# One in-place ring instead of two, and a TensorE loop with register addresses

## The chip, the cores and the metric

The kernel runs on one core of a Trainium2 chip. The core has five engines with instruction streams of their own, which meet only through semaphores: TensorE (PE) multiplies matrices, VectorE (DVE) and ScalarE (ACT) copy and compute, GpSimd (POOL) and SyncE (SP) here mostly issue transfers. Transfers between the chip's main memory and the on-chip memory run on 16 DMA engines that all queues share. The metric is the time of one execution on the device in microseconds, the median of several runs; lower is better.

## The reference

With the kernel size k = 1, the grouped convolution is a small matrix product for every pixel:

```python
H = W = 512; G = 4; Cg = 48; C = 192
x: (1, 512, 512, 192) bfloat16      w: (1, 1, 4, 48, 48) bfloat16
out[b, h, w, g, d] = sum over c of x[b, h, w, g, c] * w[0, 0, g, c, d]
```

That is 262,144 pixels of 192 channels in four groups of 48. Input and output have 100.7 MB each.

## The kernel before, in words

**Layout.** Pixels are laid out on the 128 partitions of the on-chip memory. A *column* is one pixel per partition, 384 bytes in each, so the input is about 2,056 columns. Four columns are a *group* g, two groups a *pair*. Nearly all columns lie in fields of 128 rows, where every partition reads one long run of main memory (`FULL`). Two narrow fields (`PARTIAL`, `UNEVEN` in `FRONT`) have only 120 rows, moved in several blocks of 16, 44, 12 and 32 rows, some issued by SyncE or ScalarE (the queue called "sync") and some by GpSimd. [...] Tiny transfers (`filler`, lines 282 to 287) stand between GpSimd's blocks[...].

**Two rings.** `ring` holds 240 columns of input in three slots of 80 (`BIG`, `SLOTS`), `oring` 280 columns of output. `plan_pieces` cuts the input into loads of 80 columns (8, 24 and 48 at the start), `plan_stores` the output into stores of about 70 (smaller at the end: 28, 24, 20, 16, 8).

**TensorE** (lines 322 to 397). For each pair, `transposes(pair)` turns two groups around, 12 transposes of 128x128 into `xT_ps`, each a weight load from `ring` and a matmul with the identity. `matmuls(pair)` multiplies the turned data by the weights, 12 matmuls into `o_ps`. `step(pair)` does the transposes of the next pair, then the matmuls of this one. Nine pairs are written out, then a hardware loop (line 392) turns 8 times over 30 pairs, which is one whole turn of the ring, so that every address in its body is a constant; the rest is written out again. Before the first group of a slot PE waits for the load's semaphore (line 344) and takes its 16 off again with a later transpose (line 353).

**VectorE** copies each turned pair from `xT_ps` to `xT_sb` (line 409). **ScalarE** copies each group's result from `o_ps` to `oring` (line 446), issues the stores (line 427) one group late, and waits, before it writes over a place in `oring`, until the store that read it has landed (lines 416 to 420 and 444).

**SyncE** (lines 311 to 320) issues the loads in order; before each it waits for the transposes that free its slot (`freed`, line 264). **GpSimd** (lines 268 to 309), after making constants, does the blocks of the two narrow fields: it waits for the transposes, issues the loads, waits until all of them have landed, tells PE by one increment of the slot's semaphore (line 300), and later issues the stores of the field.

Of the kernel before, what the change touches and what calls it, by code (L numbers as in the profile page):

```python
# [24 lines left out]
BIG = 80  # L25
SLOTS = 3
RCOLS = SLOTS * BIG
OGRID = (72, 140, 212, 280)
OCOLS = OGRID[-1]
HEAD = (8, 24, 48)  # L30
LATE_COLS = 240
LATE_PART = 40
LAST_PARTS = (24, 20, 16, 8)
NXP = 4
NXS = 3
NOB = 4
NTOK = 6

FULL = (("sync", 0, 128, 128, 0),)

# [4 lines left out]
UNEVEN = (("sync", 0, 16, 4, 16), *PARTIAL[1:])  # L45
FRONT = ((6, ((48, PARTIAL), (32, FULL))), (11, ((48, UNEVEN), (32, FULL))))

# [4 lines left out]
class Field:  # L52


    def __init__(self, cols, blocks, g0, pix):
        self.cols, self.g0, self.g1 = cols, g0, g0 + cols // 4
        self.full = blocks is FULL
        self.blocks = []
        for (queue, r0, rows, outer, less) in blocks:
            self.blocks.append((queue, r0, rows, outer, pix, cols - less))  # L60
            pix += rows * (cols - less)
        self.pix_end = pix
        assert cols % 4 == 0


class Piece:

    def __init__(self, i, field, c0, size):
        self.i, self.field = i, field
        self.c0, self.c1, self.size = c0, c0 + size, size  # L70
        self.g0, self.g1 = field.g0 + self.c0 // 4, field.g0 + self.c1 // 4
        self.at = 4 * self.g0 % RCOLS
        self.full, self.blocks = field.full, field.blocks
        assert size % 4 == 0 and self.at + size <= RCOLS


class Store:

    def __init__(self, field, c0, c1, at):
        self.field, self.c0, self.c1, self.at = field, c0, c1, at  # L80
        self.g0, self.g1 = field.g0 + c0 // 4, field.g0 + c1 // 4


def plan_fields(npix):

    parts, head = [], sum(HEAD)
    for slots, special in FRONT:
        parts += [(head + BIG * slots, FULL), *special]
        head = 0
    cols = npix - sum((n - b[4]) * b[2] for n, blocks in parts for b in blocks)  # L90
    if cols < 128 * BIG:
        parts, cols = [], npix
    assert cols % 512 == 0
    fields, g, pix = [], 0, 0
    for n, blocks in [*parts, (cols // 128, FULL)]:
        fields.append(Field(n, blocks, g, pix))
        g, pix = fields[-1].g1, fields[-1].pix_end
    assert pix == npix
    return fields


def plan_pieces(fields):
    pieces = []
    for f in fields:
        first = [f.cols]
        if f.full:
            first = list(HEAD) if not f.g0 and sum(HEAD) <= f.cols else []
        c = 0
        while c < f.cols:
            n = first.pop(0) if first else min(BIG, f.cols - c)  # L110
            pieces.append(Piece(len(pieces), f, c, n))
            c += n
    return pieces


def plan_stores(fields):
    total = 4 * fields[-1].g1
    stores, at = [], 0
    for f in fields:
        c = 0  # L120
        if not f.full and at + f.cols > OCOLS:
            at = 0
        ends = []
        if f is fields[-1] and f.cols > LATE_COLS:
            ends = [f.cols - sum(LAST_PARTS[i:]) for i in range(len(LAST_PARTS))]
        while c < f.cols:
            if f.full:
                end = min([g for g in OGRID if g > at + 24] or [OCOLS]) - at + c
                if f.cols < BIG:
                    end = min(OCOLS - at + c, f.cols)  # L130
                if ends and c >= f.cols - LATE_COLS:
                    end = min(OCOLS - at, LATE_PART) + c
                end = min([end, f.cols] + [e for e in ends if e > c])
            else:
                end = f.cols
            stores.append(Store(f, c, end, at))
            c, at = end, (at + end - c) % OCOLS
    return stores


class Unit:


    def __init__(self, pieces):
        self.pieces, self.g0, self.g1 = pieces, pieces[0].g0, pieces[-1].g1
        self.slot = pieces[0].at // BIG
        self.regular = pieces[0].at % BIG == 0 and 4 * (self.g1 - self.g0) == BIG


def plan_units(pieces):  # L150
    units, rest = [], list(pieces)
    while rest:
        n = 1
        if rest[0].g0 and rest[0].at % BIG == 0:
            while n < len(rest) and rest[n].at % BIG:
                n += 1
        units.append(Unit(rest[:n]))
        rest = rest[n:]
    return units


def loop_spans(units):

    body, out, run = RCOLS // 4, [], []
    for u in units + [None]:
        if u and u.regular:
            run.append(u)
            continue
        if run:

            first = max((run[0].g0 - 1) // 2, 1)
            rounds = (run[-1].g1 - 2 * first - 2) // body
            if rounds > 1:
                out.append((first, body // 2, rounds))
        run = []
    return out


def bass_standalone__grouped__vision_kernel(nc, x, w, out):
# [3 lines left out]
    assert npix % 512 == 0, "the pixel count must be a multiple of 512"  # L183

    fields = plan_fields(npix)
    pieces = plan_pieces(fields)
    stores = plan_stores(fields)
    units = plan_units(pieces)
    unit_of = {g: u for u in units for g in range(u.g0, u.g1)}
    store_of = {g: s for s in stores for g in range(s.g0, s.g1)}  # L190
    NG = pieces[-1].g1
    NP = (NG + 1) // 2
    LOOPS = loop_spans(units)
    assert all(RCOLS // 4 % n == 0 for n in (2 * NXS, 2 * NTOK, NXP))

# [4 lines left out]
    def groups(pair):  # L200
        return range(2 * pair, min(2 * pair + 2, NG))

    def transfers(ap, tile, part, queues):
        f, c0, c1, at = part.field, part.c0, part.c1, part.at
        for n, (queue, r0, rows, outer, pix, cols) in enumerate(f.blocks):
            if queue not in queues:
                continue
            px = ap[pix:pix + rows * cols, :]
            if f.full:
                view = px.rearrange("(p i) n -> p (i n)", p=rows)[:, c0 * C:c1 * C]  # L210
            else:
                assert (c0, c1) == (0, f.cols)
                view = px.rearrange("(c a i) n -> a c (i n)", a=outer, c=rows // outer)
            yield n, view, tile[r0:r0 + rows, at * C:(at + (c1 - c0 if f.full else cols)) * C]

    ld_key, unit_keys = {}, {}
    for u in units:
        whole = u.regular and len(u.pieces) == 1 and u.pieces[0].full  # L220
        for p in u.pieces:
            for n in range(len(p.blocks)):
                ld_key[p.i, n] = ("slot", u.slot) if whole else ("piece", p.i, n)
        unit_keys[u] = [("slot", u.slot)] if u.regular else [ld_key[p.i, n] for p in u.pieces for n in range(len(p.blocks))]
    mixed = [u for u in units if u.regular and unit_keys[u] != [ld_key[u.pieces[0].i, 0]]]

    with ExitStack() as es:
        block = es.enter_context(nc.Block())
        ring = es.enter_context(nc.sbuf_tensor("ring", [128, RCOLS * C], BF16))
        oring = es.enter_context(nc.sbuf_tensor("oring", [128, OCOLS * C], BF16))  # L230
# [5 lines left out]
        fill = es.enter_context(nc.sbuf_tensor("fill", [FILL_ROWS, 32 * max(1, len(mixed))], BF16))  # L236
# [6 lines left out]
        ld_sem = {k: sem("ld_" + "_".join(map(str, k))) for k in sorted({*ld_key.values(), *sum(unit_keys.values(), [])}, key=str)}  # L243
        st_sem = [[sem(f"st{i}_{n}") for n in range(len(s.field.blocks))] for i, s in enumerate(stores)]
# [3 lines left out]

        e_done = [sem(f"e_done{i}") for i in range(NTOK)]
        fa_done = [sem(f"fa_done{i}") for i in range(2 * NTOK)]  # L250
        fin = sem("fin")
        go_sem = sem("go_sem")
        fill_sem = [sem(f"fill{k}") for k in range(4 * len(mixed))]

        def columns(g):
            at = 4 * g % RCOLS
            return ring[:, at * C:(at + 4) * C]

        def out_columns(g):
            s = store_of[g]  # L260
            at = s.at + 4 * (g - s.g0)
            return oring[:, at * C:(at + 4) * C]

        def freed(p):

            return max(0, -(-(4 * p.g1 - RCOLS) // 8))

        @block.gpsimd
        def _(gp):
# [12 lines left out]
            def filler():  # L282
                k = len(used)
                src = xf[0:2 * FILL_ROWS, 0:4].rearrange("(t p) n -> p t n", t=2)
                dst = fill[:, 8 * k:8 * k + 8].rearrange("p (t n) -> p t n", t=2)
# [3 lines left out]
            for nth, u in enumerate(mixed):  # L289
                part = [p for p in u.pieces if not p.full]  # L290
                for p in part:
                    gp.wait_ge(t_done, freed(p))
                    for n, dram, sbuf in transfers(xf, ring, p, ("pool",)):
                        if n in FILL_BEFORE:
                            filler()
# [185 lines left out]
```

## Time and profile before

| | |
|---|---|
| three runs | 477.57, 477.81, 478.01 us; median 477.81 |
| the profiled execution | 477.92 us, its span 476.1 us |
| copies of results, ScalarE, line 446 | 514 of 801 ns |
| copies of turned pairs, VectorE, line 409 | 257 of 958 ns |
| loads of 80 columns, SyncE, line 320 | 22 of 3,840 KB, 26.0 us from issue to landing (median) |
| stores of 68 and 72 columns, ScalarE, line 427 | 21, 39.6 and 39.5 us to landing |
| last load issued, last store issued | 412.4 us, 467.8 us |
| chain that ended last | PE 48%, DMA 39%, ACT 8% |

Times in the profile count from the start of the span. PE is TensorE's matmul side and PEld its weight loads, which overlap; ACTq, SPq and POOLq are the queues' own instructions. Durations of matmuls include their pipeline, so a busy PE is not a PE at its peak rate. The chain of work mixes engines where several follow each other closely, so it is read together with the occupancy of the DMA engines. Transfers in flight take far longer from issue to landing than their bytes would alone, because several share the engines.

### The profile page before, as it was taken

What the parts mean: (1) busy time and instruction counts of PE and PEld (TensorE: products, weight loads), DVE (VectorE), ACT (ScalarE), POOL (GpSimd) and SP (SyncE); (2) the same over time, 40 slices, a digit from 0 to 9 for tenths busy, and PEclk for the clock granted to TensorE, in tenths of its full rate; (3) what the DMA queues carried; (4) which work ended last, traced back from release to release, by engine and by line L of the source; (5) the groups of instructions that cost most, each with busy time, mean ns of one, the idle gap of its engine ahead of it and who ended that gap; (6) DMA issues with size and microseconds to landing.
All of it is one profiled execution on the core that took longest, in us unless ns stands there. A gap on an engine that the chain in (4) does not pass through costs nothing.

```text
span 476.1 us, 13580 instructions
## 1 busy us (share of the span) xinstructions
PE 431.7 (91%) x6178; PEld 389.5 (82%) x6178; DVE 246.8 (52%) x258; ACT 388.3 (82%) x515; POOL 12.5 (3%) x28
## 2 busy tenths in 40 slices
PE   5999999999598999999998896999978979999991
PEld 5888888888597988888987796898877977988880
DVE  2655555555255555555554453555535545555550
ACT  2898899988477898999987785899968968988882
POOL 1000000200002000000000000200002000000000
PEclk9999999999889999999999997999989989999996
DMA  8999999999999999999999999999999999999996
GB/s 330 439 394 431 429 423 432 432 430 428 435 431 429 434 421 435 435 429 433 439 431 428 428 436 433 424 427 434 433 434 424 439 422 425 433 432 432 420 424 287
DMA packets 10674, 201.57 MB, mean 423 GB/s; under 512 B 2112, under 2 KB 2112, under 8 KB 2752
## 3 DMA queue, kind: packets, MB, share of 16 engines
q1 hardware_dynamic: 4320, 97.44, 48.0%
q10 hardware_dynamic: 5120, 97.42, 47.8%
q0 software_dynamic: 1216, 6.49, 3.3%
q8 instruction: 9, 0.15, 0.1%
q14 instruction: 9, 0.07, 0.0%
HBM read 100.68 MB, written 100.66 MB: 423 GB/s over the span
## 4 chain that ended last, share of the span: by engine, by line
PE 48%; DMA 39%; ACT 8%; ACTq 1%; issue 1%; another core or an unknown queue 1%; SPq 0%; POOLq 0%
DMA out_dram<-oring 29%; PE o_ps L370 28%; PE xT_ps L350 20%; DMA ring<-in_x_dram 9%; ACT oring L446 8%; ACTq L427 1%; SPq L320 0%; SPq L313 0%; ACTq L420 0%; POOLq L300 0%; POOLq L299 0%; ACTq L429 0%
## 5 line engine op out<-in xcount | busy, mean ns | idle before, releaser
L446 ACT CAST oring<-o_ps 128x768 bf16<-128x768 f32 x514 | 387.0, 801 | 78.6 <-PE o_ps L370 56.7
L409 DVE COPY xT_sb<-xT_ps 128x1536 bf16<-128x1536 bf16 x257 | 246.1, 958 | 214.8 <-PE xT_ps L350 214.8
L370 PE MATMUL o_ps<-wt,xT_sb 128*128 128x144 bf16 (+1 forms) x3084 | 289.5, 236 | 24.2 <-ACT oring L446 18.5
L370 PEld LDWEIGHTS o_ps<-wt,xT_sb 128*128 128x128 bf16 x3084 | 212.6, 99 | 63.2 <-ACT oring L446 54.3
L350 PE MATMUL xT_ps<-ident,ring 128*128 128x128 bf16 x3084 | 222.4, 222 | 7.9 <-POOLq L300 4.9
L350 PEld LDWEIGHTS xT_ps<-ident,ring 128*128 128x128 bf16 x3084 | 190.1, 100 | 10.9 <-POOLq L300 5.1
L286 POOL DMA_DIRECT2D fill<-in_x_dram x8 | 4.6, 573 | 350.5 <-PE xT_ps L350 233.1
L296 POOL DMA_DIRECT2D ring<-in_x_dram x6 | 3.3, 559 | 0.0
L307 POOL DMA_DIRECT2D out_dram<-oring x6 | 3.3, 556 | 0.0
L332 PE MATMUL o_ps<-w_sb,esel 48*128 48x48 bf16 x10 | 0.6, 210 | 2.7 <-DMA w_sb<-in_w_dram 2.7
L332 PEld LDWEIGHTS o_ps<-w_sb,esel 48*128 48x128 bf16 x10 | 0.5, 113 | 2.7 <-POOL esel L273 2.7
L402 DVE CAST wt<-o_ps 128x480 bf16<-128x480 f32 x1 | 0.7, 658 | 3.3 <-PE o_ps L332 3.3
L446 ACT ACT_TABLE_LOAD x1 | 1.3, 1283 | 0.8 <-PEq L466 0.8
L273 POOL TENSOR_SCALAR_AFFINE_SELECT esel<-esel 48x272 bf16<-48x272 bf16 x1 | 0.4, 402 | 0.0
L270 POOL MEMSET esel<- 48x272 bf16 x1 | 0.3, 317 | 0.3 <-POOLq L466 0.3
L277 POOL TENSOR_SCALAR_AFFINE_SELECT ident<-ident 128x128 bf16<-128x128 bf16 x1 | 0.3, 282 | 0.0
L271 POOL MEMSET ident<- 128x128 bf16 x1 | 0.2, 198 | 0.0
L466 POOL MEMSET const-float32-0.0<- 128x1 f32 x1 | 0.1, 98 | 0.3 <-issue 0.3
L466 POOL MEMSET const-bfloat16-1.0<- 128x1 bf16 x1 | 0.1, 101 | 0.0
L466 POOL MEMSET const-uint8-127<- 128x1 uint8 x1 | 0.1, 101 | 0.0
L466 POOL MEMSET const-float32-1.0<- 128x1 f32 x1 | 0.1, 98 | 0.0
## 6 DMA issues: line engine op xcount, KB each, us to landing
ring<-in_x_dram SPq DMA_DIRECT2D x22, 3840.0 KB, 26.0
out_dram<-oring ACTq DMA_DIRECT2D x11, 3456.0 KB, 39.5
out_dram<-oring ACTq DMA_DIRECT2D x10, 3264.0 KB, 39.6
out_dram<-oring ACTq DMA_DIRECT2D x3, 1920.0 KB, 21.1
out_dram<-oring ACTq DMA_DIRECT2D x1, 3840.0 KB, 44.7
ring<-in_x_dram SPq DMA_DIRECT2D x2, 1536.0 KB, 32.8
out_dram<-oring ACTq DMA_DIRECT2D x2, 1536.0 KB, 40.8
out_dram<-oring ACTq DMA_DIRECT2D x1, 2880.0 KB, 37.2
```

Of the source, the lines that this page charges most:

```text
L273: gp.affine_select(out=esel[:], in_=esel[:], pattern=[[-1, ECOLS]], compare_op=AluOpType.is_equal, fill=0.0, base=ESHIFT, channel_multipli ...
L286: gp.dma_start(dst, src).then_inc(fill_sem[k], 16)
L296: gp.dma_start(sbuf, dram).then_inc(ld_sem[ld_key[p.i, n]], 16)
L307: gp.dma_start(dram, sbuf).then_inc(st_sem[i][n], 16)
L332: last = pe.matmul(o_ps[:, NOB - 1, col:col + CG], lhsT=esel[:, s0:s0 + 128], rhs=w_sb[:, g, :], start=True, stop=True, skip_group_check=True)
L350: last = pe.transpose(xT_ps[:, g % NXP, j * 128:(j + 1) * 128], xg[:, j * 128:(j + 1) * 128], ident[:])
L370: last = pe.matmul(o_ps[:, v % NOB, c0_:c1_], lhsT=xs[:, j * 128:(j + 1) * 128], rhs=wt[:, WOFF[tc]:WOFF[tc] + (c1_ - c0_)], start=(tc == ...
L402: dve.tensor_copy(wt[:], o_ps[:, NOB - 1, 0:WCOLS]).then_inc(wc_sem, 1)
L409: dve.tensor_copy(xT_sb[pair % NXS][:, 0:n * 2 * UC].rearrange("p (g c) -> p g c", g=n), xT_ps[:, b0:b0 + n, 0:2 * UC]).then_inc(e_done[pa ...
L427: act.dma_start(dram, sbuf).then_inc(st_sem[i][n], 16)
L446: act.copy(out_columns(g).rearrange("p (u c) -> p u c", u=2), o_ps[:, v % NOB:v % NOB + 2, 0:UC]).then_inc(fa_done[g % (2 * NTOK)] if g < ...
L466: nc = _bacc.Bacc("TRN2", target_bir_lowering=False, num_devices=1)
```

## The change

- **One ring in place.** `ring` has 512 columns. ScalarE writes each result over the input columns that it came from, and the stores read it there; `oring` is gone. A load of columns a0 to a1 may start when the stores of the columns 512 before have landed: `wait_stored`, on SyncE and, for its blocks, on GpSimd. ScalarE no longer waits for stores, and PE's transposes no longer release loads.
- **The plan.** Four laps of 512 columns after a first field of 8 columns. Loads and stores are cut at the same places, mostly 104 columns (60 or 96 beside a narrow field or at the end of a lap). The narrow fields are 44 columns at 512 and 1536; the uneven block has 20 columns less instead of 16. From column 1440 on the stores are about 52 columns, the last ones 36, 28, 20 and 12.
- **The PE loop.** Everything from pair 0 on runs in one loop of 4 laps by 4 bodies of 128 columns (16 pairs). The place of the body in the ring is taken from the inner loop's register, so each transposed input has a register address; the PSUM and `xT_sb` addresses are constants. `NXS` is 4 instead of 3, `NTOK` 4 instead of 6.
- **Tokens.** PE cannot wait for a different load in each turn of the loop. GpSimd waits for the loads in order and increments one of 8 token semaphores for every 16 columns that have landed, at most 8 tokens ahead of PE; PE waits for a token before every second pair. The special loads and stores of the narrow fields stand in the same stream of GpSimd, at the tokens given by `SPECIAL`.

```diff
+RING = 512
+LAPS = 4
+FIRST = 8
+BODY = 128
+TOKEN = 16
+NT = BODY // TOKEN
+FIRST_CUTS = (0, 24, 104, 208, 312, 416)
+CUTS = (0, 104, 208, 312, 416)
+LATE_FROM = 1424
+LATE_PART = 52
+LAST_ENDS = (1988, 2016, 2036)
...
+UNEVEN = (("sync", 0, 16, 4, 20), *PARTIAL[1:])
+SPECIAL = ((512, 44, PARTIAL, 300), (1536, 44, UNEVEN, 250))
...
+        def wait_stored(eng, p):
+            for s in stores:
+                if s.a0 < p.a1 - RING and s.a1 > p.a0 - RING:
+                    for one in st_sem[s.i]:
+                        eng.wait_ge(one, 16)
...
+            seen = set()
+            for k in range(TOKENS):
+                for nth, (a0, cols, _, ahead) in enumerate(SPECIAL):
+                    if k == (a0 - ahead) // TOKEN + NT:
+                        special_loads(a0)
+                    if k == (a0 + cols) // TOKEN + NT + 3:
+                        special_stores(a0, nth)
+                for p in loads:
+                    if p.a0 < (k + 1) * TOKEN and p.a1 > k * TOKEN and p.i not in seen:
+                        seen.add(p.i)
+                        for one in ld_sem[p.i]:
+                            gp.wait_ge(one, 16)
+                if k >= NT:
+                    gp.wait_ge(t_done, (k - NT) * TOKEN // 8 + 2)
+                gp.sem_inc(tok[k % NT], 1)
...
         def _(sp):
             sp.dma_start(w_sb[:], wv).then_inc(w_sem, 16)
-            seen = 0
-            for p in pieces:
-                if freed(p) > seen:
-                    seen = freed(p)
-                    sp.wait_ge(t_done, seen)
+            for p in loads:
+                wait_stored(sp, p)
                 for n, dram, sbuf in transfers(xf, ring, p, ("sync",)):
-                    sp.dma_start(sbuf, dram).then_inc(ld_sem[ld_key[p.i, n]], 16)
+                    sp.dma_start(sbuf, dram).then_inc(ld_sem[p.i][n], 16)
...
+            def transposes(pair, src, token=None):
+                for g in (2 * pair, 2 * pair + 1):
                     if g % 2 and pair:
                         pe.wait_ge(e_done[(pair - 1) % NTOK], 1)
+                    if g % 2 == 0 and token is not None:
+                        pe.wait_ge(tok[token], 1)
+                    for j in range(6):
+                        e = g % 2 * 2 * UC + j * 128
+                        last = pe.transpose(xT_ps[:, g % NXP, j * 128:(j + 1) * 128], src[:, e:e + 128], ident[:])
+                        if g % 2 == 0 and token is not None and j == 2:
+                            last.then_inc(tok[token], -1)
                 last.then_inc(t_done, 1)
...
+            with pe.Fori(0, LAPS):
+                with pe.Fori(0, RING // BODY) as nth:
+                    body = ring[:].rearrange("p (b e) -> p b e", e=BODY * C)[:, bass.ds(nth, 1), :]
+                    body = body.rearrange("p b e -> p (b e)")
+                    for q in range(BODY // 8):
+                        transposes(q + 1, body[:, q * 8 * C:(q + 1) * 8 * C], q * 8 // TOKEN if q * 8 % TOKEN == 0 else None)
+                        matmuls(q)
+            matmuls(NP - 1)
...
             for g in range(NG):
                 act.wait_ge(mm_done, g + 1)
-                while todo and stores[todo[0]].g1 <= g - 1:
+                while todo and todo[0].a1 <= col(g - 1):
                     issue(todo.pop(0))
-                if over[g] is not None:
-                    landed(over[g])
                 v = 2 * g
-                act.copy(out_columns(g).rearrange("p (u c) -> p u c", u=2),
+                act.copy(columns(g).rearrange("p (u c) -> p u c", u=2),
```

## The prediction

> **What bounds the kernel now.** I read the busy table and the 40 slices first, then the DMA queues, the windows by stage, the waits, one stretch of the timeline, and last the line of the loop's own register work.
>
> ```profile
> span 476.1 us, 13580 instructions
> PE 431.7 (91%) x6178; PEld 389.5 (82%) x6178; DVE 246.8 (52%) x258; ACT 388.3 (82%) x515; POOL 12.5 (3%) x28
> ...
> DMA  8999999999999999999999999999999999999996
> ...
> q1 hardware_dynamic: 4320, 97.44, 48.0%
> q10 hardware_dynamic: 5120, 97.42, 47.8%
> q0 software_dynamic: 1216, 6.49, 3.3%
> ```
>
> PE is busy 91% of the span, but the DMA row is at nine tenths or more in 38 slices of 40, and the three data queues (loads, stores, GpSimd's) fill 48.0 + 47.8 + 3.3 = 99% of the 16 DMA engines. In the windows the last two columns are the DMA share and GB/s:
>
> ```profile
> 0.00:12.00 12.00, 6.43 (x64) 6.07 (x65) 2.75 (x4) 2.88 (x3) 1.32 (x8) 1.00 0.84 328
> ...
> 34.00:250.00 216.00, 205.51 (x2988) 185.52 (x2986) 118.91 (x125) 186.84 (x250) 5.68 (x10) 0.98 1.00 431
> 250.00:462.00 212.00, 194.12 (x2764) 175.13 (x2762) 110.14 (x115) 173.42 (x232) 5.50 (x10) 0.97 1.00 429
> 462.00:476.00 14.00, 4.08 (x55) 3.21 (x52) 1.92 (x2) 5.18 (x7) 0.00 (x0) 0.75 0.74 311
> ```
>
> The transfers are saturated from 34 to 462 us; only the first and the last dozen microseconds have room. Engine waits cost nothing as long as transfers stay queued:
>
> ```profile
> SPq L320 <- PE xT_ps L350: 398.2, 25, 25.3
> ...
> ACT oring L446 <- DMA out_dram<-oring: 15.2, 7, 3.4
> PEld xT_ps L350 <- POOLq L300: 5.1, 1, 5.1
> ```
>
> How fast could compute go? The timeline of weight loads at full speed shows the period:
>
> ```profile
> 20.70 0.72 PEld L350 LDWEIGHTS xT_ps<-ident,ring 128*128 128x128 bf16 x12
> 21.37 0.90 PEld L370 LDWEIGHTS o_ps<-wt,xT_sb 128*128 128x128 bf16 x12
> 22.26 0.72 PEld L350 LDWEIGHTS xT_ps<-ident,ring 128*128 128x128 bf16 x12
> ```
>
> In the same timeline the pattern repeats every 3.27 us per two pairs (ScalarE copies start at 15.51, 18.78, 22.04): 1.635 us per pair of groups, that is per 8 columns. 257 pairs need 420 us. The transfers' 201.57 MB at 429 to 431 GB/s take about 469 us, 1.83 us for each of the same 257 pairs. So compute has 0.19 us per pair to spare. That margin is what the change can spend.
>
> **What the Trainium skill says.** "DMA: Bandwidth & Descriptors", section "Where 436 GB/s comes from": 16 ports give 435.2 GB/s. The trace agrees: 429 to 431 GB/s in the two long windows. The same page, "Issuing engines are not separate DMA queues": queues of all issuers share the same 16 engines; the 99% above agrees, so shifting bytes between queues buys nothing. "Runtime: NRT & Kernel Launch", section "Instruction fetch mechanics": PE holds 2,048 instructions, fetched in 16 KiB blocks. The trace has nine 16 KiB instruction packets, seven before 72 us and two after 457 us, none while the loop turns; so a body of 30 pairs (30 x 48 = 1,440 matmuls and weight loads) runs without fetches, and a shorter one will.
>
> **The change part by part.**
>
> *Bytes.* The same: 100.7 MB in, 100.7 MB out. Both kernels have 2,056 columns; the two fields of 120 rows are 44 columns wide instead of 48. One DMA engine is spared in these fields: it carries 2,056 - 88 = 1,968 instead of 1,960 columns. The packet records show why: about one packet in sixteen is slow (27,648-byte stores about 1,096 instead of 1,025 ns), never two at once, so one engine. Eight more columns are 8 x 8 rows x 384 B x 2 = 49 kB, at 27.2 B/ns 1.8 us for that engine; its 96 spared columns were worth 22 us against about 19 us of slowness, so it had some 3 us to give. Bound: 0 to +1.8; I take 0.
>
> *Packets.* In the records a 30,720-byte row takes 1,138 ns and a 3,072-byte row 121 ns: 27.2 B/ns and 8 ns per packet. Full 128-row loads fall from 28 to 22 and full stores from 35 to 30: 11 x 128 = 1,408 row packets and 11 x 16 completion packets (9 ns) fewer. (1,408 x 8 + 176 x 9) / 16 = 0.80 us saved on every engine. Bound: nothing, if rows of 39,936 B are split (nothing in before is longer than 30,720), to -0.8. I take -0.8.
>
> *Start.* The first load stays 8 columns, the second 24; the third is 80 instead of 48, so PE waits some 4 us more at column 24. Loads of 520 instead of 240 columns are queued without a wait, which covers it: no DMA engine idles. 0. The dent to 386 GB/s between 26 and 34 us, as the first stores start, may be repeated or not: -1 to +0.5, taken 0.
>
> *Load waits.* SP waits for stores to land (24 loads, up to two stores each) in place of transposes; behind the waiting SP are only later loads. ScalarE loses its 15.2 us of waits on stores, which were covered. Transfers run dry only if loads wait for stores and stores for compute at once. A lap of 512 columns lasts 512 x 469 / 2,056 = 117 us. A piece needs its own load at half rate (104 x 0.23 = 24 us), its compute (13 pairs, 21 us), its store (24 us) and a few us of landing: 73 of 117, the rest is queue. So a dry queue is not the likely case. With before's landing times scaled to 104 columns (26.0 x 104/80 + 39.5 x 104/70 = 92) plus 21, a lap is 113 of 117: the margin thins, but those times include queueing.
>
> *Tokens.* GpSimd issues 128 increments in place of PE's own waits. An event instruction on its queue took 43 ns; two in a row after each landing add about 0.1 us to each of 24 loads, under the spare of PE. Behind GpSimd's waits stand the two sets of special transfers and all later tokens; the first special loads come after token 20, which needs the load that ends at column 416, at about 59 us, and are needed at about 112 us. 0; without the cover some 3 us.
>
> *The loop.* Each of 12 transposes per pair now takes its address from a register, so I expect one register addition and one register-addressed weight load each: 3,072 of either. This is the unknown that matters. Nearest rows:
>
> ```profile
> L392 PEldq ALU_OP  x8: 36/36/42, 73.6 to 452.2; - x8
> L392 PEldq COMPARE_BRANCH  x8: 76/208/235, 73.7 to 452.3; - x8
> ```
>
> An addition lasts 36 ns, and the branch behind it starts 101 ns after it. In the records the next weight load starts 56 ns after the taken branch, and the sequencer ran ahead of the array: ten queued instructions hid the 0.34 us of addition and branch. Low end: 12 x (36 + 25) = 0.73 us plus 0.11 for the matmuls (twelve were issued within 56 ns of a wait ending): 0.84, hidden, cost 0. High end: 12 x (101 + 62) + 0.11 = 2.07 us per pair, where 62 ns is what "TensorE: Matmul & The Clock Gate", "Wait — 56ns, not 53.3ns?", gives for a matmul decoded in software; I take it for a register-addressed load, and no run here shows it. The middle, 1.45 us, is under the 1.83 of the transfers. I take 0. The 16 branches at 0.2 us are 3.3 us at most, spread over spare time. Below nothing: fewer fetches save nothing, since no fetch shows during the rounds.
>
> *End.* The last parts are 36, 28, 20, 12 columns instead of 28, 24, 20, 16, 8. At the end 8 columns took 8 packets of 121 ns on the last engine, ended at 475.2; 12 take 8 x 177. +0.4 if the last store sets the end, -0.5 if the ragged last 6 us close up because compute ends earlier. 0.
>
> Sum: -0.80 against the profiled execution's 477.92 us (span 476.1 and 1.8 around it): 477.1. The median of the three runs is 0.1 lower, so **477.0 us**.
>
> **The rivals.**
>
> *A (forecast), 46%: the transfers go on binding*, 475.4 to 478.2.
>
> *B, slower, 32%: PE's sequencer becomes the bound.* Place: the register addition and register-addressed load ahead of each transpose. Then time = 7.5 (first transposes) + 257 x p + about 7 (last copies, last store, around the span). It equals 477.0 at p = 1.80 us; from there every 0.1 us costs 25.7. Between 1.80 and 2.07 lies 477 to 546; in the middle 510. For it: both instructions are of a kind that before has only 8 times. Against: the sequencer was seen ahead of the array.
>
> *C, slower or same, 16%: the ring runs dry* because a load waits for a whole landed store of up to 104 columns on the slowest DMA engine. If a lap takes 118.5 instead of 117 us, 3.5 laps lose 5 us: 482. Against: 73 of 117 above. A late end from the spared engine (478.7) is counted here.
>
> *D, faster, 6%: the dent at 26 us and the ragged end also go*, 2 us more: 475.
>
> **How the numbers follow.** This measurement can tell about 0.2% from no change, so faster means under 476.86 and slower above 478.77. A lies across that border: 0.20 faster, 0.24 same, 0.02 slower. With B (0.32 slower), C (0.14 slower, 0.02 same) and D (0.06 faster): faster 0.26, same 0.26, slower 0.48. The forecast's own range is 475.4 to 478.2; for 8 in 10 it reaches from 475 (0.03 below) to 505, which leaves about half of B outside.
>
> **What would show it.** Right: the DMA row at nine tenths from the second to the last slice but one, some 9,100 packets instead of 10,674, no instruction packets for PE after the start, PE idle on tokens of GpSimd. B: the DMA share in the long windows falls under 0.98, PE never waits for a load late in the run, weight loads of transposes stand over 80 ns apart instead of 0.72 / 12 = 60. C: SP and PE both wait for DMA while the share dips. The forecast fails if register-addressed loads take over 1.8 us per pair.

## The result, and the profile after

| | before | after |
|---|---|---|
| median of the runs (us) | 477.88 | 544.28 |
| lowest to highest (us) | 477.57 to 478.01 | 544.23 to 544.33 |
| span of the profiled execution (us) | 476.1 | 542.6 |

The ratio is 1.139, 95% interval 1.137 to 1.141: the kernel is 66 us slower, far outside the forecast range of 475 to 505. Ratios here and below leave out executions over 1.5% above the fastest of their kernel; medians do not. The lines of the page that answer to those shown of before:

```profile
span 542.6 us, 16801 instructions
...
PE 523.7 (97%) x6178; PEld 443.6 (82%) x6178; DVE 246.7 (45%) x258; ACT 389.0 (72%) x515; POOL 12.5 (2%) x28
...
DMA  8999999999999979989999899899799999544475
...
q1 hardware_dynamic: 3456, 97.71, 44.1%
q10 hardware_dynamic: 4400, 97.69, 43.0%
q0 software_dynamic: 1216, 5.95, 2.6%
```

The bytes are the same, but the three queues now fill 44.1 + 43.0 + 2.6 = 90% of the DMA engines' time instead of 99%, and late in the run the row drops to 4 and 5. PE does the same 6,178 matmuls and is busy 524 us instead of 432. The windows say it by stage (DMA share and GB/s are the last two columns):

```profile
20.00:150.00 130.00, 129.95 (x1536) 110.27 (x1535) 60.67 (x65) 96.66 (x128) 2.93 (x5) 0.99 1.00 417
...
250.00:460.00 210.00, 209.07 (x2479) 176.79 (x2479) 98.63 (x104) 155.55 (x207) 5.50 (x10) 1.00 0.96 398
460.00:540.00 80.00, 76.60 (x911) 64.68 (x909) 36.35 (x38) 58.88 (x78) 0.00 (x0) 1.00 0.53 222
```

Until 150 us the transfers run full; my reading is that they live on the 520 columns that are loaded without a wait. After that they follow PE's pace. The last load lands at 457 us; from 460 us only stores are left, as fast as PE makes results, and the engines are half idle. PE waits for almost nothing. The waits list has

```profile
DVE xT_sb L314 <- PE xT_ps L265: 285.6, 257, 5.9
...
ACT ring L336 <- PE o_ps L281: 143.5, 250, 8.4
...
PE xT_ps L265 <- POOLq L231: 6.2, 2, 4.3
```

VectorE and ScalarE wait for PE, and PE waited for tokens twice, 6.2 us in all (4.3 of them at the start). So PE is the bound. What it does is seen in the timeline (start, duration, engine):

```profile
199.93 0.96 DVE L314 COPY xT_sb<-xT_ps 128x1536 bf16<-128x1536 bf16 x1 [1.06 <-PE xT_ps L265]
...
200.50 1.24 PEld L265 LDWEIGHTS xT_ps<-ident,ring 128*128 x12
...
201.65 0.84 PEld L281 LDWEIGHTS o_ps<-wt,xT_sb 128*128 128x128 bf16 x12
...
201.91 0.96 DVE L314 COPY xT_sb<-xT_ps 128x1536 bf16<-128x1536 bf16 x1 [1.02 <-PE xT_ps L265]
```

Twelve transposes take 1.24 us instead of 0.72, the twelve matmuls 0.84 against 0.90, and the copies follow each other every 1.98 to 2.01 us: that is the time per pair. The line of the transposes has the instruction that before had not:

```profile
L265 PEldq FUSED_REGOPS  x3072: 46/46/46, 8.0 to 534.3; - x192
```

One operation of 46 ns on PE's sequencer for each of the 3,072 transposes in the loop. In the records of one pair, the first six loads still follow each other 56 ns apart, as they do in before: their operations were worked off during the matmuls. The last six stand behind the wait for VectorE's copy. There each load follows 95 ns after the start of its operation and the next operation 28 ns after the load: 123.5 ns for each of these transposes.

The sum is complete. The first copy starts at 6.3 us and the last at 534.6; behind it come 7.9 us of span and 1.7 around it. Of the 528.3 between, 256 x 2.01 = 514.6 is the steady pair; the start (pairs 0 to 3, waiting for the third load) adds 7.8, fifteen jumps back 4.6, two stalls further on (at 162 and 422 us) 2.9, and the shorter pairs take off 1.6.

### The profile page after: what moved, and what is told of

The parts are those of the page before. It is cut to its first block, busy times and chain, and to the rows that moved or that the text cites. A ratio compares the mean times of both kernels' runs of the same rounds, so it can differ in the third digit from the quotient of the medians.

```text
span 542.6 us, 16801 instructions
## 1 busy us (share of the span) xinstructions
PE 523.7 (97%) x6178; PEld 443.6 (82%) x6178; DVE 246.7 (45%) x258; ACT 389.0 (72%) x515; POOL 12.5 (2%) x28
## 2 busy tenths in 40 slices
DMA packets 9085, 201.49 MB, mean 371 GB/s; under 512 B 1936, under 2 KB 1936, under 8 KB 2576
## 3 DMA queue, kind: packets, MB, share of 16 engines
q1 hardware_dynamic: 3456, 97.71, 44.1%
## 4 chain that ended last, share of the span: by engine, by line
PE 94%; DMA 3%; ACT 1%; ACTq 1%; SPq 0%; issue 0%; POOLq 0%
PE xT_ps L265 55%; PE o_ps L281 39%; DMA ring<-in_x_dram 3%; ACT ring L336 1%; ACTq L323 0%; SPq L241 0%; SPq L237 0%; ACTq L325 0%; POOLq L231 0%
## 5 line engine op out<-in xcount | busy, mean ns | idle before, releaser
L336 ACT CAST ring<-o_ps 128x768 bf16<-128x768 f32 x514 | 387.7, 801 | 148.5 <-PE o_ps L281 143.5
L265 PE MATMUL xT_ps<-ident,ring 128*128 128x128 bf16 x3084 | 347.7, 225 | 7.9 <-POOLq L231 6.2
L265 PEld LDWEIGHTS xT_ps<-ident,ring 128*128 (+1 forms) x3084 | 250.2, 97 | 86.1 <-issue 9.1
L281 PE MATMUL o_ps<-wt,xT_sb 128*128 128x144 bf16 (+1 forms) x3084 | 258.1, 234 | 2.9 <-ACT ring L336 2.6
L281 PEld LDWEIGHTS o_ps<-wt,xT_sb 128*128 128x128 bf16 x3084 | 217.1, 98 | 4.6 <-ACT ring L336 3.9
L200 POOL DMA_DIRECT2D out_dram<-ring x6 | 3.3, 556 | 0.0
```

The source lines that it names most:

```text
L200: gp.dma_start(dst, src).then_inc(done, 16)
L265: last = pe.transpose(xT_ps[:, g % NXP, j * 128:(j + 1) * 128], src[:, e:e + 128], ident[:])
L281: last = pe.matmul(o_ps[:, v % NOB, c0_:c1_], lhsT=xs[:, j * 128:(j + 1) * 128], rhs=wt[:, WOFF[tc]:WOFF[tc] + (c1_ - c0_)], start=(tc == ...
L336: act.copy(columns(g).rearrange("p (u c) -> p u c", u=2), o_ps[:, v % NOB:v % NOB + 2, 0:UC]).then_inc(fa_done[g % (2 * NTOK)] if g < NG - ...
```

## The experiments

Theory 1: the register operation is the cause, by the place where it stands. Rivals: the wait alone; the register-addressed load; tokens; the ring in place. "Pair" below is the median distance between the starts of VectorE's copies in the trace (1.70 us in before, 2.01 after). All ratios are to the kernel before, run on the same chip.

### Where the wait stands

In both kernels the wait for VectorE's copy of the pair before, `e_done`, stands between the first six and the last six transposes. Two kernels move it.

```diff
-                    if g % 2 and pair:
-                        pe.wait_ge(e_done[(pair - 1) % NTOK], 1)
...
             def matmuls(pair):
-                if pair + 1 == NP:
-                    pe.wait_ge(e_done[pair % NTOK], 1)
+                pe.wait_ge(e_done[pair % NTOK], 1)
```

> The wait for VectorE's copy is taken from the middle of the transposes and put ahead of the matmuls that need the copy; register addresses and all else stay. Theory 1 (a serial loop: copy of a pair 1.0 us, then six transposes that are 123 ns apart behind the wait, then the next copy): with the wait gone from there PE's sequencer needs 12 x 0.123 + 0.2 = 1.7 us per pair, under the 1.80 of the transfers, so the time falls to 477 to 480 us. Theory 2 (PE's sequencer is simply full: 2.0 us per pair wherever the wait stands): 540 to 545 us.

Measured 526.57 us, ratio 1.101 [1.100, 1.103]; pair 1.92. Neither theory's figure: moving the wait takes 18 of the 66 us away. The pairs alternate between 1.72 and 2.09 us. In 78 of 256 the first operation starts within 16 ns of a matmul load that had waited for ScalarE's copy; these pairs take 2.11 us, and the next ones 1.71. So there the operations stand behind ScalarE's wait instead of VectorE's. That this is all of the rest is not shown; no run removes it.

```diff
-                    if g % 2 and pair:
+                    if g % 2 == 0 and pair:
```

> The same wait moved ahead of all 12 transposes of a pair instead of the last six; nothing else. Theory 1: all 12 then stand in the serial loop, 1.0 + 12 x 0.123 + 0.25 = 2.73 us per pair, 257 of them and 17 us at the ends are about 715 us. Theory 2: unchanged, 540 to 550 us.

Measured 732.27 us (one execution; 715 was expected), pair 2.77. Ahead of all twelve, the copy and twelve slow transposes are in series; six transposes more behind the wait cost 0.76 us per pair, 6 x 123.5 ns = 0.74. That is the series of theory 1.

### Which part of the register addressing costs

First the loops written out, every address a constant, tokens and ring in place kept:

```diff
-            with pe.Fori(0, LAPS):
-                with pe.Fori(0, RING // BODY) as nth:
-                    body = ring[:].rearrange("p (b e) -> p b e", e=BODY * C)[:, bass.ds(nth, 1), :]
...
+            for nth in range(LAPS * RING // BODY):
+                body = ring[:].rearrange("p (b e) -> p b e", e=BODY * C)[:, nth % (RING // BODY), :]
```

> The two loops are written out, so that every address is a constant and no register operation is left; ring, tokens, stores and waits as in the changed kernel. If the register addresses are the whole cost, as theories 1 and 2 both say: 476 to 478 us, and 477.0 if the saved packets count as forecast. Theory 3 (the tokens of GpSimd or the in-place ring cost the time): over 500 us. Some 12,400 PE instructions are fetched then; if these fetches stall PE, 480 to 490 us.

Measured 499.06 us (494.9 to 504.0), ratio 1.042 [1.037, 1.046]; pair 1.70 as in before. 45 of the 66 us are gone with the registers. 21 are not: a second loss, which the slow PE had covered.

Then the addressing without most of its operations. All six transposes of a group read the same first 128 elements (five sixths of the input are left unread, so the output is no longer the convolution, and only time and trace are of use); so one operation serves six loads that are all register-addressed:

```diff
-                        last = pe.transpose(xT_ps[:, g % NXP, j * 128:(j + 1) * 128], src[:, e:e + 128], ident[:])
+                        last = pe.transpose(xT_ps[:, g % NXP, j * 128:(j + 1) * 128], src[:, e - e % (2 * UC):e - e % (2 * UC) + 128], ident[:])
```

> All six transposes of a group read the same first 128 elements of the group, so five sixths of the input is not used; the address is then computed once per group (512 register operations instead of 3,072), while all 3,072 weight loads keep a register address. If the register operation makes the 123 ns: transposes about 60 ns apart after the first of a group, 1.7 us per pair or less, 477 to 480 us. If a weight load with a register address is itself slow: still 95 to 123 ns apart, 1.8 to 2.0 us per pair, 480 to 545 us.

Measured 502.94 us (495.1 to 508.3), pair 1.64, with

```profile
L265 PEldq FUSED_REGOPS  x512: 46/46/46, 8.2 to 490.0; - x171
```

The total misses the expected 477 to 480, but the pair decides: it is as short as theory 1 said. The total is near that of the loops written out, and as there PE waits for tokens (40.5 us in all): the second loss. A load that takes its address from a register costs nothing that shows; the operation that makes the address does.

### The register alone, in the kernel before

Here nothing else of the change is present: two rings, no tokens, bodies of 30 pairs.

```diff
+                    with pe.Fori(0, 1) as zero:
+                        base = ring[:].rearrange("p (b e) -> p b e", e=RCOLS * C)[:, bass.ds(zero, 1), :]
...
+                            step(pair, base)
```

> The kernel before with its own two rings, waits and bodies of 30 pairs; only the transposes in the loop take their input address from a register (of an inner loop of one turn, so its value is always 0). 240 of 257 pairs are touched. Theory 1 (the register operation ahead of each transpose, with VectorE's copy in series behind the last six, makes 2.0 us per pair wherever it stands): 240 x 2.0 + 17 x 1.65 + 14 = 522 us, 516 to 528, with weight loads of transposes about 123 ns apart. Theory 2 (the register operation only hurts together with tokens and the ring in place): 478 to 490.

Measured 477.77 us, ratio 0.9995 [0.998, 1.001]. This run decides nothing: the trace has no register operation on the transposes' line, since the address had been folded into constants.

```diff
+                            if reg is not None:
+                                e = e - reg * 128 if g % 2 or j else e + reg * 128
...
+            r = pe.alloc_register()
+            pe.reg_mov(r, 0)
+            zero = pe.snap(r, min_val=0, max_val=1)
```

> The kernel before with its own two rings, waits and bodies; the register of the earlier attempt had been folded into constants, so here the transposes in the loop take their input address from a register that is set to 0 once. 240 of 257 pairs are touched. Theory 1 (the register operation ahead of each transpose, with VectorE's copy in series behind the last six, makes 2.0 us per pair wherever it stands): 516 to 528, weight loads of transposes 123 ns apart. Theory 2 (it only hurts together with the ring in place): 478 to 490.

Measured 730.61 us, ratio 1.528 [1.526, 1.531], pair 2.68: far over the expectation, and the line of the transposes says why.

```profile
L353 PEldq FUSED_REGOPS  x2880: 47/51/69, 24.4 to 709.0; - x192
L353 PEldq MOVE  x2640: 29/29/34, 24.5 to 708.8; - x189
```

The subtraction takes two operations for each transpose, and loads stand 217 ns apart. Twelve times 0.217 is 2.60 us: here the sequencer's throughput is the bound. In the records of one pair VectorE's copy ends at 302.52 us, and the operation that waits for it starts only at 302.62, behind the operations before it. With an address of the form register plus constant (`e = e + reg * 128`) there is one:

> As the last kernel with the register in the kernel before, but with addresses of the form register plus constant, so that each transpose in the loop has one register operation instead of the two (a move and a fused operation) that the last one turned out to have; body of 30 x 60 = 1,800 instructions. Theory 1 (one operation ahead of each transpose puts weight loads 123 ns apart, and with VectorE's copy in series behind the last six a pair takes 2.0 us, in the two-ring kernel too): 516 to 528. Theory 2 (what costs is the length of the body that is fetched anew, or the ring in place): weight loads 123 ns apart but pairs of 1.70 to 1.85 us, 478 to 492.

Measured 583.72 us, ratio 1.223 [1.219, 1.228]; pair 2.03, as theory 1 said, and the total is not. Most of the rest is the jump back. First the queue of instruction packets on the page (packets, MB, share), then the branch of the loop (shortest, median, longest ns):

```profile
q8 instruction: 73, 1.20, 0.8%
```

```profile
L398 PEldq COMPARE_BRANCH  x8: 76/4888/8602, 85.4 to 561.7; - x8
```

The longer body is fetched anew in every round (73 instruction packets against 9), and PE stands still for 4.4 to 8.5 us at each of the seven jumps back. With the copies right behind them the jumps cost some 46 us, of the 62 that the run took over 522. So the last pair of runs kept the body shorter, with six operations per pair, once ahead of the wait and once behind it:

```diff
-                            if reg is not None and e + 128 < RCOLS * C:
+                            if reg is not None and g % 2 == 0:
```

```diff
-                            if reg is not None and e + 128 < RCOLS * C:
+                            if reg is not None and g % 2 and e + 128 < RCOLS * C:
```

> The kernel before; in the loop only the first six transposes of each pair, which stand ahead of the wait for VectorE's copy, have one register operation each. Theory R (the sequencer works off these operations while the array still does the matmuls, and what costs is only operations behind that wait): pairs of 1.70 to 1.75 us at the median, 477 to 485, more only by stalls where the loop jumps back (some 6 us a round) if the longer body of some 1,620 instructions is fetched anew. Rival S (the sequencer's throughput sets the time, 123 ns per operation wherever it stands): the same time as with the operations behind the wait.

> The same with only the last six transposes of each pair, those behind the wait, having one register operation each. Theory R: VectorE's copy, the wait and six transposes 123 ns apart stay in series, so pairs of 2.0 us at the median and 516 to 528, with the same addition for fetches if there is one. Rival S: as with the operations ahead of the wait.

Measured 477.84 us (ratio 0.999 [0.998, 1.000]) ahead of the wait and 525.24 us (ratio 1.098 [1.095, 1.100]) behind it; both show 9 instruction packets. The transposes' line and the loads of one pair, first of the kernel with the operations ahead:

```profile
L353 PEldq FUSED_REGOPS  x1440: 42/46/60, 24.4 to 451.3; - x180
```

```profile
203.04 0.76 PEld L353 LDWEIGHTS xT_ps<-ident,ring 128*128 x12
```

then of the kernel with the operations behind:

```profile
L353 PEldq FUSED_REGOPS  x1432: 46/46/60, 24.0 to 503.8; - x179
```

```profile
202.78 1.24 PEld L353 LDWEIGHTS xT_ps<-ident,ring 128*128 128x128 bf16 x12
```

Nearly the same count of the same operation costs nothing on one side of a wait and 47 us on the other. Pairs are 1.73 and 2.00 us. Theory R holds, S falls at this count.

### The second loss: 21 us without any register

All these start from the kernel with the loops written out (499.06 us). First without tokens, PE waiting for the loads itself:

```diff
-                        pe.wait_ge(tok[token], 1)
+                    for p in loads:
+                        if pair and p.a0 == col(g):
+                            for one in ld_sem[p.i]:
+                                pe.wait_ge(one, 16)
```

> The kernel with the loops written out and constant addresses, and without tokens: PE waits for the loads themselves; GpSimd keeps only its special transfers. Theory A (the 21 us that the written-out kernel lost come from tokens, which stand behind GpSimd's own waits for stores): 478 to 484. Theory B (they come from the ring in place: a load waits for a landed store of 104 columns, and packets take longer): no change, 494 to 504, and PE waits for loads in place of tokens for 30 to 40 us.

Measured 500.44 us, ratio 1.049 [1.043, 1.054]. Without registers tokens cost nothing that shows; PE waits for loads instead:

```profile
PE xT_ps L254 <- DMA ring<-in_x_dram: 35.4, 9, 11.6
```

Then smaller stores, then smaller loads too:

```diff
-LATE_FROM = 1424
+LATE_FROM = 104
...
-    return cut(fields, ends), cut(fields, ends | late | set(LAST_ENDS))
+    return cut(fields, ends | late), cut(fields, ends | late | set(LAST_ENDS))
```

> The kernel with the loops written out and constant addresses, with the stores cut at 52 columns from column 104 on instead of from 1440 on; loads and tokens as they were. Theory B1 (the ring runs dry because a load waits for a whole landed store of 104 columns that was issued late): the first half of each store leaves about 10 us earlier, so 481 to 490 and fewer long stalls of PE. Theory B2 (the loss is in packets that take longer than their bytes, whatever the dependence) or A (tokens): 494 to 504.

> The kernel with the loops written out and constant addresses, with loads as well as stores cut at 52 columns. Theory B1 (what is left of the loss, 9 us with stores of 52, is that a load still waits for both halves of the column range and PE for a whole load of 104): 478 to 483, PE's waits for tokens under 10 us in sum. Rival (the 9 us are the price of more packets, instruction fetches and the end): 485 to 489.

Measured 486.74 us (ratio 1.018 [1.014, 1.023]) with the first line alone and 484.51 us (1.014 [1.011, 1.016]) with both. Finer stores take away 12 of the 21 us, finer loads 2 more. The finer stores change two things at once: a load waits for a shorter store to land, and packets that were slow no longer are (below). The runs don't separate the two. PE's waits for tokens, with loops written out, with stores of 52, and with loads of 52 too:

```profile
PE xT_ps L265 <- POOLq L231: 37.0, 9, 11.9
```

```profile
PE xT_ps L265 <- POOLq L231: 16.3, 6, 5.1
```

```profile
PE xT_ps L265 <- POOLq L231: 23.1, 12, 3.6
```

With both cut, the expected 478 to 483 was missed, and so was the expectation of under 10 us of waits: they rose again, to 23.1. Of the remaining 6 us, the queues of the finest cuts hold 13,594 packets instead of 10,674, 2,920 x 8 ns / 16 = 1.5 us by before's packet cost, and the instruction packets of the written-out loop take 0.6% of the engines, 2.9 us against 0.5 in before. The rest is not told apart.

The DMA engines of the written-out kernel lost the 22 us of span in two ways: packets filled 97.7% of 498.2 us, 487, against 99.3% of 476.1, 473. So 14 us are longer packets (2 of them more instruction packets), and 8 are idle time. Of its 1,280 store packets of 39,936 bytes, 38% lasted over 3% longer than their bytes, 1,581 ns in the mean instead of 1,476. Is that their size?

```diff
-OGRID = (72, 140, 212, 280)
+OGRID = (104, 208, 280)
```

> The kernel before with stores of 104, 104 and 72 columns round its output ring instead of 72, 68, 72 and 68. Theory P (rows of 39,936 bytes are what makes packets slow: more than one slow engine in 16): these packets take over 3 per cent longer in more than 12 per cent of cases, the time is 481 to 486. Rival (packets are slow for another reason, of the ring in place): at most 7 per cent of them are slow, 477 to 480.

Measured in the two-ring kernel: eleven executions from 480.7 to 497.0 us, median 490.5 against 478.0; the three quickest give ratio 1.012 [1.007, 1.016]. So stores of 104 columns cost this kernel 3 to 19 us too. In the traced execution (495.1 us) 8.8% of the packets of that size were slow, against 6% of the stores' in before. That is under the 12% of theory P and over the 7% of its rival, and neither is confirmed; but the size alone does not give 38%. With stores of 52 columns it is 7%. Nor do slow packets need the ring in place: in the two-ring kernel with one operation for each transpose (583.72 us), 20% of the load packets of 30,720 bytes were slow, against 2% in before. Why they are slow stays open, also whether they cause a dry queue or come with it.

### Both repairs, and one alone

> The changed kernel, register and loops as they are, with loads and stores cut at 52 columns. Theory 1 (the sequencer sets the time at 2.0 us per pair, the ring's loss is covered by it apart from a few stalls): 537 to 545. Rival (the two losses add up): 523 to 532.

The changed kernel with finer cuts and its registers kept: 545.34 us, ratio 1.140 [1.138, 1.142]. The ring's loss was covered by the slow PE; mending it alone gains nothing. Last, a loop whose body is the whole ring, so that every address is a constant though it is still a loop:

```diff
-                with pe.Fori(0, RING // BODY) as nth:
...
+                for q in range(RING // 8):
+                    transposes(q + 1, ring[:, q * 8 * C:(q + 1) * 8 * C], q * 8 // TOKEN % NT if q * 8 % TOKEN == 0 else None)
+                    matmuls(q)
```

> The changed kernel with one loop of 4 laps whose body is the whole ring (64 pairs), so that every address is a constant, and loads and stores of 52 columns; tokens kept. Theory 1 (only the register operation, not the loop or the tokens, slows PE): within 3 us of the written-out kernel with the same cuts. Rival (the jump back over a body that has to be fetched anew costs): slower than that by over 3 us.

Measured 485.00 us, ratio 1.015 [1.013, 1.017]: within 0.5 us of the written-out kernel with the same cuts. The loop costs nothing that shows, though PE stalls some 6.6 us at each of its three jumps back (19.7 us in the waits list). No version tried is faster than the kernel before.

## Why the prediction was wrong

**The step that failed is "The loop".** It added up the operations, 12 per pair, compared the sum with 1.83 us of transfers, and put the cost at 0. The measured unit, 123.5 ns, lies between its two ends (61 and 163 ns; the 25 in the low end has no source there), and 12 x 0.1235 + 0.11 = 1.59 us is under 1.80. By that sum the forecast would have held. What it left out is a series that was already in before, and that its trace showed:

```profile
18.36 0.96 DVE L409 COPY xT_sb<-xT_ps 128x1536 bf16<-128x1536 bf16 x1 [0.75 <-PE xT_ps L350]
19.92 0.96 DVE L409 COPY xT_sb<-xT_ps 128x1536 bf16<-128x1536 bf16 x1 [0.60 <-PE xT_ps L350]
```

Copies at best 1.56 us apart: the copy (0.96), the release of the wait (0.05), six loads of transposes (0.24 from the first to the sixth), and 0.31 to the next copy's start. No instruction in that ring can run ahead. The register adds 67.5 ns to each of the six: 1.56 + 6 x 0.0675 = 1.97 us, and 2.0 was measured. Six operations behind a wait decide, the six ahead of it are free; the two kernels with six each show this.

The records show the mechanism. In before the wait stands on a weight load, and as soon as it is released the loads behind it follow, most of them 56 ns apart. In the changed kernel it stands on a register operation; the copy ends at 200.88 us, the operation starts at 200.92, and the five others follow one by one. The Trainium skill, "Perfetto Trace Analysis", section "Per-engine timelines", says that a matmul or weight load is pushed to a wait queue, after which the sequencer decodes on, while an instruction of the sequencer itself holds it through its wait. The trace agrees with the second half: no operation behind the waiting one starts before it. It limits the first half, and before showed that already. "The sequencer ran ahead of the array" was the argument against rival B, taken from the additions at the end of the loop (73.6 us is the first):

```profile
73.56 0.38 PEld L370 LDWEIGHTS o_ps<-wt,xT_sb 128*128 128x128 bf16 x6 [0.23 <-ACT oring L446]
```

These loads had waited for ScalarE's copy. The addition comes eleven loads and matmuls later in the program, and it started 13 ns after the first of the six; all eight additions started 11 to 13 ns after such a load. So the sequencer was ahead of the array, but not ahead of a wait. With VectorE's wait moved (526.57 us) that shows again: its series is gone, and in 78 pairs the operations begin right behind a load that had waited for ScalarE. Two operations per transpose make the throughput alone the bound (2.68 us per pair).

**The estimate of 62 ns** taken from the skill for a register-addressed load was the wrong item: the load costs nothing extra (512 operations, 3,072 such loads: 1.64 us per pair). The threshold itself, 1.80, fits the runs: at 1.73 us nothing is lost, at 1.92 it is.

**The rivals.** B named the right engine, the right instruction, the weight loads' distance (over 80 ns) and the falling DMA share (0.93 and 0.96 between 150 and 460 us); its high end gave 546. That this is close to 544.28 is luck: it comes of twelve operations of 163 ns, where six of 123.5 in a ring with the copy set the time. It had 32%, and the range cut off at 505, inside B. C came true under cover: with PE at its old speed the ring does run dry, 21 us. In "Load waits" the estimate of 73 us for a piece's round was the wrong one of two: issue to landing took 48.2 us for a load and 41.5 for a store in the written-out kernel, with 21 of compute 111 of the 117 us of a lap, as the "113 of 117" there had said. A is right only for tokens (0 was taken, and without registers none is seen) and for packets (9,085 against "some 9,100"; 39,936-byte rows are not split, 1,476 ns). The 0.8 us of "Packets" can't be seen in any total. In "Bytes", slow packets that come "never two at once, so one engine" are not what the records say: of 219 store packets over 10,000 bytes that took 3 to 20% longer than their bytes, 43 began while another was under way. No run tests that term.

**The jumps** were 0.2 us in the prediction and 0.3 in the trace, but with PE as the bound they count: 4.6 us. So does the third load, which the transfers no longer hide: 7.8 us at the start.

## What to carry to other kernels

Before adding instructions to a sequencer, look in the trace for the closed ring of waits that the engine stands in (here copy, wait, transposes, copy), and count only what lies in that ring, at full price: its period, not the sum of busy time, has the margin. In these kernels an address from a register cost one or two sequencer operations for each distinct address; put them ahead of the wait in the ring that sets the time, or make the loop's body as long as the ring so that addresses are constants. In a ring in place, the piece of a store is the piece of the next load's wait: try finer stores first (12 us here, against 2 for finer loads on top).

## What was not expected of the hardware

- A loop body counted at 30 x 60 = 1,800 PE instructions was fetched anew in each round, nine packets of 16 KiB every time, with PE at a stand for 4.4 to 8.5 us at each jump; bodies of 1,440 and some 1,620 were not. The Trainium skill, "Runtime: NRT & Kernel Launch", section "Instruction fetch mechanics", gives PE 2,048 instructions in blocks of 256. By that, 1,800 are a little over seven blocks and should fit. The nine that are fetched, 2,304 instructions by my estimate from the page's figures, do not; why there are nine stays open.
- An operation of PE's sequencer started only behind a matmul load that waited, eleven instructions ahead of it: 11 to 13 ns after it at all eight loop ends of before.
